# Packed attention with a gated convolution on one core: the same instructions in another written order

## The chip, the cores and the metric

The kernel runs on one core of a Trainium2 chip. The metric is the time of one execution in microseconds (us) as the device measures it. Three runs of the kernel before took 318.8, 318.99 and 320.42 us; the median is 318.99 us. A further execution was profiled; its span from the first to the last instruction is 317.6 us.

The engines are named as the profile names them: PE is the matrix engine, PEld its loading of weights, DVE the vector engine, ACT the scalar engine, POOL the general engine, SP the engine that issues the DMAs.

## The reference, cut to what matters

```python
scale = 1 / sqrt(64)                  # 8 batches, 8 heads, 576 rows, 64 columns a head; p has 32 rows
def sm_attn(qq, kk, vv):
    s = scale * matmul(qq, kk.T)
    a = exp(s - max(s)); a = a / (sum(a) + 1e-9)
    return matmul(a, vv)
pp  = sm_attn(p, k, v)                # 32 rows a head
x   = heads side by side of sm_attn(q, pp, pp)          # 576 x 512 a batch
gate = sigmoid(sum over t of conv_w[t] * x shifted back by 4 - t rows)     # 5 taps
out = (gate * (x @ w_val)) @ w_out
```

The three weight arrays come in as float64 and are turned into float32 on the chip.

## The kernel before, in words

All work is on 8 batches, one after another, each in two groups of four heads (g). The work of a batch is cut into streams, Python generators that each issue one small piece of work per step. A stream has a letter, and the batch follows it:

- `K`, `V`, `Q`, `P` issue the loads of k, v, q (two DMAs a batch, one per group, 0.59 MB each; tiles `km`, `vm`, `qm`) and of p (two small DMAs). `L` loads the weights: eight DMAs for `w_val` (0.26 MB each, tile `wv_words`), one for the taps, four for `w_out` (0.52 MB each, `wo_words`).
- `W`, `C`, `O` turn the weights from double words into float32, with ACT, DVE and POOL.
- `k` and `q` turn k and q on PE (three groups of four transposes for each g, `kpt` and `qpt`), and ACT copies them out of PSUM.
- `a` is the attention of p: scores `s` from `kT` and `pT`, a maximum (`nb`), the exponential, transposes `at`, and products `pv` with v, giving `ppd`. `p` turns `ppd` (`ppTt`).
- `s`, `t` are the second attention's scores `s` (from `qT` and `ppT`) and softmax, giving `a2`; `w` is `wp`, the product of pp with `w_val`; `x` (function `mixed`) makes the attention's output in the columns of the convolution.
- `g` (function `gate`) is the convolution: for each of four blocks of columns ACT multiplies the first tap, then DVE adds four taps, each a SCALAR_TENSOR_TENSOR that reads and writes the same tile `sig`; ACT takes the tanh.
- `v` (function `value`) makes `val` on PE, DVE multiplies it by the gate, and `gvh`/`gvl` hold the high and low part of the result. `o` (function `project`) is the product with `w_out`: 12 matmuls of 512 columns a chunk of 128 rows, and the store.

The products of `s` and `wp` use the matrix engine as eight tiles of 64 rows by 32 columns, those of `x` as tiles of 32 by 64, those of `pv` as 128 by 32. All others (transposes, `val`, `o`) use the full 128 by 128 array.

Nothing is left to a scheduler. The table `ORDER` (line 46) is a list of tokens, each a stream, its batch and a number of steps (`k0.4` is four steps of turning k of batch 0), and `run` (line 602) takes them one after another. The class `InOrder` (line 82) ties each instruction behind the one issued before it on its engine. The token list is therefore the order of every engine's queue, and of the DMAs on SP. All instructions are issued in line 90 in the kernel before, and in line 86 in the changed one, whose table is four lines shorter; groups in the profile are told apart by their tiles.

Two resources tie the streams together. PSUM holds two buffers `big` (used by `s`, `wp`, `x`, `val`), three `mid` (transposes, `pv`) and one `out`; the load buffers hold one batch of k, v and q each (two tiles, one per g), so a load of the next batch waits until the tile has been read. The sign `|` in the table ends the staging of the weights.

Of the kernel before, what the change touches and what calls it, by code (L numbers as in the profile page):

```python
# [45 lines left out]
ORDER = """
x0 L0.5 P0 W0.2 K0 W0 K0 W0 Q0 W0 P1 W0.3 V0 L0 W0 V0 Q0 W0.5 C0 L0 k0 W0 k0 P2 C0 W0 C0 W0 k0 C0 W0 C0 k0.4 K1
W0 C0 L0 k0.2 W0 k0.2 C0 W0 a0 k0 C0 W0 k0 a0 k0 K1 q0 W0 a0.2 W0 k1 q0.2 a0 k1 P3 q0.2 a0.3 L0 a0.2 Q1 a0 q0
a0.3 O0 V1 a0.7 O0 a0 O0 a0 O0.2 a0 p0 V1 O0.2 p0 O0 s0 O0 q0 w0 s0 q0 O0 s0 q0 O0 w0 s0 O0 w0 s0 q0.2 Q1 O0 t0
k1 q0 s0 k1 O0 k1 t0 s0 k1.2 K2 O0 k1 a1 t0 O0.2 s0 t0 x0 a1 O0 s0 k1 t0 a1 O0 k1.2 s0 k1.2 K2 t0 x0.2 k1 k2 P4  # L50
O0 x0 a1 O0 t0 g0 a1 q1 O0 g0 x0 a1.3 k2 g0 q1.2 a1.2 t0 q1.2 a1.2 g0 Q2 t0 x0 a1 O0 a1 q1 g0 x0.2 O0 a1 V2 g0
t0 v0 x0 O0 a1 g0 O0.2 a1 g0 q1 a1.2 O0 v0 a1.2 O0 a1 q1 g0 a1 O0.3 k2 O0 a1 p1 V2 k2.2 p1 q1 k2.2 q1 s1 g0 k2
K3 k2 O0 a2 k2 s1 k2 O0 q1 k2 a2 k2 O0.2 Q2 w1 s1 K3 q1 O0 g0 q2 s1 a2 g0 w1 O0 s1.3 w1 k2 k3 P5 O0 g0 q2.2 s1
a2 q2 x1 g0 q2 s1 | v0 a2 k3 Q3 q2 k3 v0 a2 v0 k3 s1 a2 g0 k3 a2 t1 q2 k3 a2.2 q2.2 a2 g0 a2 t1 q2 k3 v0 a2.2 k3
K4 g0 v0 k3 q2 a2 V3 k3.2 t1 Q3 g0 a2.2 g0 x1 v0 t1 g0 v0 q2 x1 t1 a2 t1 k3 x1 a2 k3 g0 t1 a2.2 x1 K4 v0 a2.2 k3
g0 v0 k4 V3 a2 a3 P6 p2 t1 p2 a3 t1 s2 v0 a3 q3 g0 q3 v0 s2 g0 x1 t1 g1 x1 v0 g1 v0 a3 x1 s2 k4 x1 g1 s2 a3 q3
k4 x1 g1 a3 q3.2 Q4 a3 w2 g1 s2 q3 v0 o0 g1 t2 g1 w2 g1 t2 k4 w2 v1 o0 g1 o0 t2 o0 g1 t2 v1 g1 v1 t2 s2 g1 x2.2
v1 g1 o0 g1 q3 a3 k4 x2 o0 s2 o0 a3 q3 g1 k4 s2 g1 s2 v1 g1 o0.2 s2 o0 v1 g1.2 t2 v1 g1 t2 a3 v1 o0 v1 a3 o0 x2
g1 a3 k4 t2 a3.2 k4 K5 v1 x2 q3 g1 a3 k4 V4 v1 a3.3 g1 k4 q3 v1.2 x2 g1 a3 q3 g2 v1 k4 a3 Q4 x2 q3 g2 v1 a3 g2
a3.2 x2 v1 x2 k4 V4 a3 g2 k4 t2 o1 K5 k4 t2 x2 g2.3 v2 o1 g2 o1 g2 a4 v2 p3 o1 p3 a4 v2 g2 a4 v2 g2 s3 o1 x3 w3  # L60
g2 o1 s3 g2 q4 s3 v2 w3 g2 s3 q4 w3 q4 o1 q4 v2 s3 g2 v2 t3 s3 o1 g2 t3 a4 o1 s3 q4 k5 o1 a4 q4 Q5 k5 g2 P7 a4.2
g2 s3 g2 t3 s3 a4 o1 k5 g2 x3 a4 o1 s3 a4 o1 t3 v2 a4 g2 x3 k5 t3 g2 v2 t3 o1.2 g2 t3 x3 v2 g2 a4 k5 a4.2 v2 t3
k5.2 v2 a4 v2 V5 k5 K6 a4 t3 x3.2 t3 a4 k5 g3 v2 x3 a4 k5 g3 k5 v2 a4 q4 g3 a4 q4 v2 o2 k5 x3 g3.2 a4 g3 x3 a4
g3 a4 x3 g3 q4 v3 V5 a4 q4 g3 o2 g3 o2.2 v3 g3 v3.2 g3 x4 g3 p4 q4 o2 g3 k5 p4 Q5 a5 k5 g3 o2 s4 q4 K6 o2 a5 s4
a5 g3 s4 g3 s4 a5 o2 w4 g3 o2 a5 g3 q5 a5.3 g3 o2 a5 g3 s4 w4 g3 q5 t4 a5 o2 s4 w4 a5 t4 k6 o2 a5 q5 k6 a5 s4 a5
q5 t4 v3 a5 V6 s4 t4 g3 s4 x4 v3 g3 q5 t4 k6 v3 Q6 s4 v3.2 q5 k6 t4 k6 x4 q5 k6.2 v3 q5 x4 t4 K7 k6 a5 v3 a5 q5
k6 t4 x4.2 q5 v3.2 t4 g4 t4 x4 a5 g4 k6 a5 k6 a5 v3 a5 x4 q5 g4 a5 x4 Q6 q5 v3 g4 k6 v3 o3 x4 g4.3 a5 o3 g4 k6
a5 a6 V6 k6 g4 o3 k7 p5 g4 o3 p5 K7 a6 g4 a6 g4 x5 a6 g4 s5 o3 g4 k7.2 o3 a6 q6 k7.2 g4 q6 o3 a6.2 s5 k7 g4 s5
v4 o3 g4 s5 o3 g4 q6 g4 v4 a6 w5 s5 g4 q6 a6 s5 t5 v4 a6 q6 w5 o3 g4 t5 Q7 q6 s5 a6 g4 q6 s5 o3 a6 k7 q6 g4 s5
o3.2 a6 k7 t5 g4 w5 t5 s5 t5 x5 o3 v4 k7 o3 t5 v4 x5 k7 t5 k7 v4 x5 k7 t5 v4 a6 x5.2 v4 x5 a6 V7 a6 g5 a6 v4 a6  # L70
g5 t5 x5 g5 a6 q6 v4 a6.2 x5 q6 g5 a6 v4 a6 t5 x5 q6 g5 a6 a7 V7 q6 Q7 v4 p6 g5 v4 a7 g5 p6 g5 a7 k7 v4 s6 k7 g5
v4 a7 q7 s6 q7.2 g5 w6 q7 v4 o4 g5 w6 a7 x6 g5 s6 a7.2 s6 w6 g5 v5 o4 g5 s6 o4 g5 s6 q7 v5 a7 o4 q7 g5 a7 v5 s6
v5 s6 v5 t6 o4 s6 o4 g5 q7 a7 o4 t6 q7 a7 s6 v5 g5 v5 t6 g5 v5.2 t6 g5 o4 t6 o4 x6 t6 a7 q7 a7 o4 x6 g5 t6 q7 v5
g5 v5 x6 o4 t6 q7 o4 v5.2 t6 g5 x6 q7 t6 x6 g5 x6 g6 v5 a7 x6 g6 x6 v5 g6 a7 x6 a7.2 v5 o5 a7 g6.2 v6 o5 g6 o5
g6 a7 o5 v6 a7 g6 v6 g6 v6.2 g6 o5.2 g6 a7 o5 g6 x7 g6 v6 a7 g6 v6 g6 a7 o5 v6 o5 g6 v6 a7 g6 p7 g6 o5 g6 v6 p7
g6 v6 g6 s7 v6 o5 v6 g6 o5 s7 g6 o5 s7 g6 s7 v6.2 w7 s7 v6 o5 t7 s7 o5 o6 w7 s7 t7 w7 t7 s7 o6 x7 t7 o6 s7 o6 t7
x7 s7 t7 x7 o6 t7 o6.2 x7.2 t7 g7 t7 g7 t7 v7 o6 g7 o6 g7 x7 g7 o6 g7.2 v7 x7 g7 v7 x7 g7 o6 v7.2 o6 x7 g7.2 o7
g7.2 v7 g7 v7 g7 v7.2 o7 g7.4 v7 g7 v7.3 o7 g7.3 o7 g7 v7.3 o7.15
"""


# [564 lines left out]
```

## Time and profile before

| | |
|---|---|
| time, median of 3 runs | 318.99 us (318.8 to 320.42) |
| span of the profiled execution | 317.6 us |
| PE busy | 284.6 us, 90% of the span, 2996 matmuls |
| DVE busy | 255.0 us, 80% |
| ACT busy | 212.7 us, 67% |
| POOL busy | 67.8 us, 21% |
| HBM read, written | 33.57 MB, 9.44 MB |

The time of the runs holds about 1.4 us more than the span of the profiled execution (318.99 less 317.6). PE's matmuls overlap, so a matmul's own duration is longer than the distance between two starts; for PE the distances between starts are read. Rows called waits give the engine and tile that stood idle, what released it, and then the sum in us, the number of waits and the longest.

### The profile page before, as it was taken

What the parts mean: (1) busy time and instruction counts of PE and PEld (TensorE: products, weight loads), DVE (VectorE), ACT (ScalarE), POOL (GpSimd) and SP (SyncE); (2) the same over time, 40 slices, a digit from 0 to 9 for tenths busy, and PEclk for the clock granted to TensorE, in tenths of its full rate; (3) what the DMA queues carried; (4) which work ended last, traced back from release to release, by engine and by line L of the source; (5) the groups of instructions that cost most, each with busy time, mean ns of one, the idle gap of its engine ahead of it and who ended that gap; (6) DMA issues with size and microseconds to landing.
All of it is one profiled execution on the core that took longest, in us unless ns stands there. A gap on an engine that the chain in (4) does not pass through costs nothing.

```text
span 317.6 us, 7342 instructions
## 1 busy us (share of the span) xinstructions
PE 284.6 (90%) x2996; PEld 209.2 (66%) x2996; DVE 255.0 (80%) x396; ACT 212.7 (67%) x432; POOL 67.8 (21%) x71
## 2 busy tenths in 40 slices
PE   0088786879989999999999999999999999999993
...
DVE  0983388679999997999789986897998977878771
...
DMA  7999999999973239533657558243702011111005
GB/s 165 216 219 254 262 240 223 217 229 188 233 150 107 68 102 238 138 95 97 151 128 196 166 135 199 85 116 103 152 33 66 35 42 60 54 70 45 33 0 166
DMA packets 42475, 43.48 MB, mean 137 GB/s; under 512 B 6085, under 2 KB 36805, under 8 KB 42442
## 3 DMA queue, kind: packets, MB, share of 16 engines
...
HBM read 33.57 MB, written 9.44 MB: 135 GB/s over the span
## 4 chain that ended last, share of the span: by engine, by line
PE 81%; ACT 8%; DMA 5%; DVE 3%; SPq 1%; issue 1%; ACTq 0%; DVEq 0%
PE o L90 32%; PE val L90 16%; PE x L90 6%; PE s L90 6%; PE kpt L90 5%; PE qpt L90 5%; PE pv L90 3%; DMA km<-in_k_dram 3%; PE at L90 3%; PE wp L90 3%; DMA wv_words<-in_moe_w_val_dram 2%; DVE sig L90 1%; ACT a1t L90 1%; ACT a L90 1%; ACT wo_top L90 1%; SPq L90 1%
## 5 line engine op out<-in xcount | busy, mean ns | idle before, releaser
L90 DVE SCALAR_TENSOR_TENSOR sig<-xp,cw,sig 128x576 f32<-128x576 f32 x128 | 106.4, 832 | 10.8 <-ACT sig L90 9.4
L90 PE MATMUL o<-woh,gvh 128*128 128x512 f32 x144 | 59.1, 411 | 0.1
L90 PE MATMUL o<-woh,gvl 128*128 128x512 f32 x144 | 56.5, 393 | 0.0
L90 PE MATMUL o<-wol,gvh 128*128 128x512 f32 x144 | 56.4, 392 | 0.0
L90 PE MATMUL val<-a2h,wph 128*128 128x288 f32 x128 | 39.4, 308 | 0.1
L90 ACT COPY osb<-o 128x512 f32<-128x512 f32 x34 | 19.8, 584 | 27.2 <-PE o L90 18.0
L90 PE MATMUL val<-a2h,wpl 128*128 128x288 f32 x128 | 37.9, 296 | 0.0
L90 PE MATMUL val<-a2l,wph 128*128 128x288 f32 x128 | 37.7, 295 | 0.0
L90 ACT ACTIVATE sig<-sig 128x576 f32<-128x576 f32 x32 | 22.0, 688 | 18.1 <-DVE sig L90 18.0
L90 POOL TENSOR_TENSOR t<-t,mx 128x576 f32<-128x576 f32 x16 | 23.1, 1442 | 47.8 <-DVE mx L90 46.6
L90 PEld LDWEIGHTS o<-woh,gvh 128*128 128x128 f32 x144 | 27.1, 188 | 9.4 <-issue 3.0
L90 POOL TENSOR_TENSOR t<-t,rs 128x576 f32<-128x576 f32 x16 | 22.0, 1372 | 50.1 <-DVE rs L90 44.6
L90 DVE SCALAR_TENSOR_TENSOR sig<-sig,val 128x576 f32<-128x576 f32 x32 | 23.9, 748 | 10.7 <-ACT sig L90 5.4
L90 PEld LDWEIGHTS o<-woh,gvl 128*128 128x128 f32 x144 | 27.1, 188 | 6.5 <-DVE gvl L90 0.4
L90 PEld LDWEIGHTS o<-wol,gvh 128*128 128x128 f32 x144 | 27.2, 189 | 4.6
L90 ACT COPY kT<-kpt 128x384 f32<-128x384 f32 x48 | 23.3, 485 | 10.2 <-PE kpt L90 10.0
L90 PE MATMUL kpt<-ident,km 96*128 96x96 f32 x192 | 26.8, 275 | 2.5 <-DMA km<-in_k_dram 2.4
L90 PE MATMUL qpt<-ident,qm 96*128 96x96 f32 x192 | 25.7, 262 | 3.2 <-ACT pT L90 1.9
L90 PEld LDWEIGHTS qpt<-ident,qm 96*128 96x128 f32 x192 | 19.6, 147 | 13.2 <-issue 7.5
L90 ACT COPY qT<-qpt 128x384 f32<-128x384 f32 x48 | 22.9, 485 | 6.9 <-PE qpt L90 6.9
L90 DVE TENSOR_TENSOR gvl<-sig,gvh 128x576 fp32r<-128x576 f32 x32 | 25.2, 788 | 2.6 <-ACT gvh L90 2.4
L90 PEld LDWEIGHTS kpt<-ident,km 96*128 96x128 f32 x192 | 21.0, 157 | 9.2 <-issue 4.9
...
## 6 DMA issues: line engine op xcount, KB each, us to landing
...
```

The source lines that it names most:

```text
L90: made = getattr(self.engine, op)(*args, **kw)
```

## The change

Only the table `ORDER` is another. The streams, the tiles, the buffers and the number of matmuls, copies and DMAs are the same. The diff is the whole table; its first lines read:

```diff
 ORDER = """
-x0 L0.5 P0 W0.2 K0 W0 K0 W0 Q0 W0 P1 W0.3 V0 L0 W0 V0 Q0 W0.5 C0 L0 k0 W0 k0 P2 C0 W0 C0 W0 k0 C0 W0 C0 k0.4 K1
+L0 K0 P0 k0.2 K0 L0 W0 k0.6 a0.2 k0.4 L0 k0 V0 k0 a0 x0 W0.9 a0.4 W0.3 a0.8 L0.2 W0.2 L0 Q0 W0.2 a0.5 W0.2 V0 q0
...
-g7.2 v7 g7 v7 g7 v7.2 o7 g7.4 v7 g7 v7.3 o7 g7.3 o7 g7 v7.3 o7.15
+v7.2 g7 o6 v7 g7 o6 g7.2 v7 g7 v7 g7.4 v7.2 g7 o6 v7.3 o7.19 o6.3
 """
```

In the lists below a row is one or more instructions that follow each other on the engine; `x8` is their number.

**SP, the start of the program.** Before:

```order
L90 DMA wv_words<-in_moe_w_val_dram 64x1024 x8
L90 DMA cw_words<-in_moe_conv_w_dram 5x1024
L90 DMA p_94<-in_p_dram 128x2x64 x2
L90 DMA km_0_100<-in_k_dram 96x4x384
L90 DMA km_1_103<-in_k_dram 96x4x384
L90 DMA qm_0_106<-in_q_dram 96x12x128
L90 DMA p_109<-in_p_dram 128x2x64 x2
L90 DMA vm_0_116<-in_v_dram 96x4x384
L90 DMA wo_words<-in_moe_w_out_dram 128x1024
L90 DMA vm_1_121<-in_v_dram 96x4x384
L90 DMA qm_1_123<-in_q_dram 96x12x128
```

Now:

```order
L86 DMA wv_words<-in_moe_w_val_dram 64x1024 x2
L86 DMA km_0_81<-in_k_dram 96x4x384
L86 DMA p_83<-in_p_dram 128x2x64 x2
L86 DMA km_1_91<-in_k_dram 96x4x384
L86 DMA wv_words<-in_moe_w_val_dram 64x1024 x4
L86 DMA vm_0_149<-in_v_dram 96x4x384
L86 DMA wv_words<-in_moe_w_val_dram 64x1024 x2
L86 DMA cw_words<-in_moe_conv_w_dram 5x1024
L86 DMA wo_words<-in_moe_w_out_dram 128x1024
L86 DMA qm_0_236<-in_q_dram 96x12x128
L86 DMA vm_1_254<-in_v_dram 96x4x384
L86 DMA wo_words<-in_moe_w_out_dram 128x1024
```

Six of the eight loads of `w_val` now stand behind the first loads of k and p, and the last two behind the first v. The last two loads of `w_out`, which stood 15th and 18th among these rows, now stand 20th and 25th.

**PE, where batch 3's `x` products stand** (`x_1_0` and `x_1_1` are the two halves of rows of group 1). Before, the two halves stand 17 rows apart, the first of them among the transposes:

```order
L90 MATMUL val_3_1966<-a2l_1277,wph_1283 128x288
L90 MATMUL at_1_0_1992<-ident,a_4_1_1837 96x128 x2
L90 MATMUL kpt_1_0_1996<-ident,km_1_1628 128x96 x4
L90 MATMUL x_1_0_2004<-a_3_1774,ppd_1243 64x288 x4
L90 MATMUL kpt_1_1_2012<-ident,km_1_1628 128x96 x4
L90 MATMUL at_1_1_2018<-ident,a_4_1_1837 96x128 x2
```

Now:

```order
L86 MATMUL at_0_2_2139<-ident,a_5_0_1863 96x128 x2
L86 MATMUL x_1_0_2148<-a_3_1778,ppd_1066 64x288 x4
L86 MATMUL x_1_1_2154<-a_3_1778,ppd_1066 64x288 x4
L86 MATMUL pv_0_2160<-vm_0_2082,a1t_0_2121 32x64 x24
L86 MATMUL s_4_1_2185<-qT_1_1981,ppT_1977 32x288 x8
L86 MATMUL qpt_0_0_2195<-ident,qm_0_2101 128x96 x4
```

The two halves stand next to each other, and `pv` and `s` follow them. Counted over PE's whole list, the array's shape changes 147 times before and 102 times now; in all 14 pairs of `x` stand directly together, where none did, and three pairs of `s` products from the same source are among the new neighbours.

**DVE, the first taps of the convolution** (`sig_1` is the second block of columns). Before:

```order
L90 RECIPROCAL sm_1_1_560<-sm_1_1_560 128x1
L90 SCALAR_TENSOR_TENSOR sig_1_660<-xp_0_78,cw,sig_1_660 128x576
L90 SCALAR_TENSOR_TENSOR sig_0_545<-sig_0_545,val_0_643 128x576
L90 SCALAR_TENSOR_TENSOR sig_1_660<-xp_0_78,cw,sig_1_660 128x576
L90 TENSOR_SCALAR wo_words<-wo_words 128x512
```

Now:

```order
L86 STREAM_TRANSPOSE a_0_399<-t_0_334 128x576
L86 SCALAR_TENSOR_TENSOR wo_top<-wo_top,wo_words 128x512
L86 TENSOR_SCALAR wo_words<-wo_top 128x512
L86 SCALAR_TENSOR_TENSOR sig_1_661<-xp_0_155,cw,sig_1_661 128x576 x4
L86 STREAM_TRANSPOSE t_1_706<-s_1_0_708 128x576
```

The four taps of a block, which had other work between them, follow each other directly. Over the whole list a tap directly follows a tap of the same block 30 times before and 55 times now.

At the end of the list, the last chunk of batch 6 (`o_3`, 12 matmuls, its copy and its store) now stands behind all of batch 7. On PE 72 matmuls of `o` follow the last `val`, where 36 did.

More of the change, by code (lines that the diff above doesn't have):

```diff
@@ L46 @@
 ORDER = """
-x0 L0.5 P0 W0.2 K0 W0 K0 W0 Q0 W0 P1 W0.3 V0 L0 W0 V0 Q0 W0.5 C0 L0 k0 W0 k0 P2 C0 W0 C0 W0 k0 C0 W0 C0 k0.4 K1
[L48 to L76, printed above, removed]
@@ L77 @@
-x7 s7 t7 x7 o6 t7 o6.2 x7.2 t7 g7 t7 g7 t7 v7 o6 g7 o6 g7 x7 g7 o6 g7.2 v7 x7 g7 v7 x7 g7 o6 v7.2 o6 x7 g7.2 o7
-g7.2 v7 g7 v7 g7 v7.2 o7 g7.4 v7 g7 v7.3 o7 g7.3 o7 g7 v7.3 o7.15
+L0 K0 P0 k0.2 K0 L0 W0 k0.6 a0.2 k0.4 L0 k0 V0 k0 a0 x0 W0.9 a0.4 W0.3 a0.8 L0.2 W0.2 L0 Q0 W0.2 a0.5 W0.2 V0 q0
+O0.8 L0 q0 Q0 W0.4 a0 q0 W0 a0 q0.2 O0.2 a0 C0 a0 C0 p0 C0 q0 p0 s0 q0 C0 s0 K1 P1 K1 Q1 O0.2 q0.3 s0 q0.2 O0 s0.2
+w0.2 O0.2 C0 t0 O0 s0 t0 O0 k1.2 O0 k1.3 w0 V1 t0 P2 k1.3 t0 k1 L0 V1 O0 k1 s0.2 C0 x0.2 k1.4 x0 t0 s0 C0 x0 C0 a1
@@ new lines @@
+s0 g0 a1.6 K2 g0 K2 a1 t0 a1.2 q1 g0 a1 g0 O0 q1.2 g0 x0 a1 q1 Q1 k2 a1 O0.2 k2 a1.2 q1.2 t0 a1 O0 a1 t0 a1.2 O0.2
+L0 a1.3 g0 a1 g0 t0 x0.2 a1 x0 p1 k2 x0 g0 p1 k2.4 g0 O0.3 k2 s1 w1.2 k2.3 g0.2 s1 K3 s1 k2 g0 P3 k2.2 a2 t0 w1 s1.2
+a2 O0 K3 q1 V2 O0 q1 a2 O0 t1 q1.4 a2 x1 a2 O0.4 v0 k3 a2 k3.4 P4 Q2 a2 t1 g0 v0 k3.2 a2 O0 t1 O0 s1 x1 k3 a2 x1
+a2.2 V2 g0 a2 s1 a2 K4 s1 O0 s1 O0.2 | g0 k3 a3.2 k3 Q2 k3.3 a3 k3 g0.2 x1 v0 a2.2 K4 v0 a2.2 v0 x1 a2 g0 a2 g0 v0
+g0 a2.2 a3 k4 g0 g1 q2 a3 v0.2 q2 a2 k4 a3.2 v0 g0 t1.2 a3.2 q2 V3 q2 a2 q2 v0 a2 s1 a3 t1 p2.2 q2 g0 a3 v0.3 k4.2
@@ new lines @@
+t1 k4 t1 k4.2 s2 g0 k4 v0 a3 K5 s2 q2 g1 a3 g1 q2.3 x1 q2.2 x1 g1.2 x1 t1.2 x1 k4 x1 k4.4 v0.2 a4 w2 a3 s2 V3 w2 K5
+a4 w2 g1.3 a4 o0 g1 o0 s2 g1 v1 o0 s2 v1 g1 Q3 v1 k4 g1 v1.2 g1 a3.2 g1 o0 v1 g1 v1 g1 P5 g1 a3 V4 a3 t2 s2 a4 o0 s2
+x2 a4 a3 P7 v1 a3.2 g1 s2 g1.2 q3 Q3 a3 o0.2 t2 v1 k5 o0.2 q3.2 a4 k5 q3 v1.2 q3.2 k5 s2 t2 k5 g1.2 a3 g1 t2 x2 a3
+x2.2 k5 x2 g1 k5 v1 k5 g2 p3 v1 P6 s2 t2 v1 k5 o0 t2 v1 k5 g2 K6 a4 q3 p3 a4 k5 V4 g2.3 a4 s3 x2 w3 o0 Q4 q3 s3.2 g2
+t2.2 g2 k5 q3 s3 q3 v1 t2 q3 t2 o1 s3 o1.2 v2 g2 k5 g2 o1 g2 v2 q3 w3.2 a4.4 g2 t3 x2.4 g2 a4 a5 o0 o1.2 s3 a4 t3 k5
@@ new lines @@
+q4 t3 q4 a5 s3 v2 a5 k5 o1 g2 x3 t3 a4.3 g2 a4.2 s3 a4.2 g2 x3.3 a4 x3 a4 q4.3 t3 q4 Q4 p4 v2.2 s3 K6 s3 p4 g2 v2
+q4.3 g3 s4 a5 t3 k6 q4.2 o1 s4 o1 k6 a5 k6 g2 k6 g2 g3 g2 t3.2 k6 g2 v2 a5 s4 o1.2 k6 v2 s4 a5 V5 g2 v2.2 g2.2 Q5 g3
+o1 v2 q4 o1 s4 a5.2 v2 a5.2 t4 a5 t3 t4 g3 x3 a5 x3.3 g3 a5 s4 q5 s4 x3 t3 g3 a5 g2 v2 v3 v2 a5 g3 k6 o1 v2 g3 q5 k6
+v3 v2 a5 k6 a5 o1 k6 g3.3 V5 w4.2 g3.2 w4 a5.3 q5 a5 q5 Q5 o2 t4 v3 x4 s4 k6.2 q5.2 k6 g3 v3 x4 o2 x4.3 g3 k6 a5 g4
+a5 a6.3 s4 Q6 g3 a6 p5.2 a6 g3 q5 t4 o2 g3 g4 k7 g4 g3.2 q5 o2 a6 o2 g3 o2 k7 g3 v3.3 g3 v3.3 g3 o2 V6 v3 o2 v3.2 t4
```

9 lines of the change are left out of this document (added).

## The prediction

> **What bounds the kernel now.** I read the page's slices first, then the busy time by stages.
>
> ```profile
> span 317.6 us, 7342 instructions
> PE 284.6 (90%) x2996; PEld 209.2 (66%) x2996; DVE 255.0 (80%) x396; ACT 212.7 (67%) x432; POOL 67.8 (21%) x71
> PE   0088786879989999999999999999999999999993
> DVE  0983388679999997999789986897998977878771
> DMA  7999999999973239533657558243702011111005
> ...
> 0.00:72.00 72.00, 46.11 (x579) 27.73 (x580) 45.77 (x76) 45.81 (x99) 28.18 (x31) 0.91 1.09 225
> 72.00:96.00 24.00, 22.22 (x322) 15.07 (x321) 23.18 (x41) 20.79 (x49) 6.48 (x6) 1.00 0.94 188
> 96.00:304.00 208.00, 207.93 (x2065) 160.16 (x2065) 181.19 (x276) 142.94 (x281) 33.17 (x35) 1.00 0.39 103
> 304.00:318.00 14.00, 8.37 (x36) 6.24 (x34) 4.87 (x7) 3.12 (x5) 0.00 (x0) 0.95 0.30 94
> ```
>
> The last four rows are windows: length, then busy us of PE, PEld, DVE, ACT and POOL, the granted clock, the DMA share and GB/s. There are three stages. Up to 72 us nobody is full but the DMA engines (share 1.09, 225 GB/s): the loads arrive one behind another and the first batches' chains are short of partners. From 72 to 96 DVE is the fullest, 23.18 of 24 us. From 96 to 304 PE works 207.93 of 208 us, so the end is set there by PE's list and by what one entry of it costs; DVE idles 26.8 us (208 less 181.19). The waits agree: what PE lost by name is at the start.
>
> ```profile
> PE pTt L90 <- DMA p<-in_p_dram: 14.1, 1, 14.1
> ACT sig L90 <- DVE sig L90: 18.0, 12, 3.3
> DVE sig L90 <- ACT sig L90: 14.7, 16, 2.0
> DVE sig L90 <- PE val L90: 5.2, 6, 2.0
> ```
>
> **Part 1: fewer changes of shape on PE.** The distance between starts tells what a change costs (timeline of PE: start, duration, count).
>
> ```profile
> 102.24 0.39 PE L90 MATMUL o<-wol,gvh 128*128 128x512 f32 x1
> 102.47 0.39 PE L90 MATMUL o<-woh,gvl 128*128 128x512 f32 x1
> 102.79 0.72 PE L90 MATMUL s<-qT,ppT 64*32 64x288 f32 x16
> 103.44 0.72 PE L90 MATMUL x<-a,ppd 32*64 32x288 f32 x8
> 104.08 0.55 PE L90 MATMUL qpt<-ident,qm 96*128 96x96 f32 x4
> ...
> 113.94 0.30 PE L90 MATMUL val<-a2h,wpl 128*128 128x288 f32 x1
> 114.08 0.29 PE L90 MATMUL val<-a2l,wph 128*128 128x288 f32 x1
> 114.30 0.71 PE L90 MATMUL x<-a,ppd 32*64 32x288 f32 x8
> ...
> 137.83 0.72 PE L90 MATMUL s<-qT,ppT 64*32 64x288 f32 x16
> 138.34 0.69 PE L90 MATMUL s<-kT,pT 64*32 64x288 f32 x16
> 138.96 0.55 PE L90 MATMUL qpt<-ident,qm 96*128 96x96 f32 x4
> ...
> L90 PE MATMUL x<-a,ppd 32*64 32x288 f32 x256 | 24.1, 447 | 0.5 <-ACT xp L90 0.5
> ```
>
> Going in: an `o` starts 0.23 after the one before it, but the `s` starts 0.32 after the last `o`; a `val` 0.14 after a `val`, but the `x` 0.22 after it. So 0.09 us. Going out: the `s` at 102.79 holds PE for 0.65 us, but the `s` at 137.83, with another `s` behind it, only 0.51. So 0.14 us. Two products put together save one way in and one way out, 0.23 us. The lists count 147 changes before and 102 now: 45 fewer, 22.5 such pairs, **5.2 us** of PE time, nearly all in the stage that PE fills. For `x` the trace has no two in a row. It runs alone in 0.64 us; one of its matmuls takes 0.447, so going out is worth between 0 and 0.19. The bounds for all: 22.5 x 0.09 = 2.0 us, and 22.5 x (0.09 + 0.19) = 6.3 us. I take what `s` shows, since `x` streams as many columns.
>
> The Trainium skill ("TensorE: Matmul & The Clock Gate", Part 3, "The mechanism") says that a weight load overlaps matmuls in flight only where the row group differs. The two `x` of a pair use the same rows, so by it a pair would save only the way in; with 14 pairs of `x` the sum would shrink by 14 x 0.14 = 2.0 us. The two `s` above also use the same rows and do save 0.14 us, so here the trace speaks against applying it to this case.
>
> **Part 2: the loads' order.** The chain of waits has two loads from issue to landing; the timeline shows who used them.
>
> ```profile
> 3.26 6.08 DMA wv_words<-in_moe_w_val_dram
> 9.35 9.81 DMA km<-in_k_dram
> ...
> 20.00:26.00 6.00, 6.00 (x56) 3.70 (x55) 3.84 (x9) 2.74 (x7) 1.29 (x1) 1.00 1.13 258
> 26.00:32.00 6.00, 4.89 (x116) 3.37 (x114) 2.04 (x7) 5.25 (x16) 0.80 (x1) 1.00 1.15 234
> ...
> 16.69 2.18 PE L90 MATMUL kpt<-ident,km 96*128 96x96 f32 x12 [1.98 <-DMA km<-in_k_dram]
> 31.17 0.43 PE L90 MATMUL pv<-vm,a1t 96*32 96x64 f32 x16 [0.41 <-ACT a1t L90]
> 32.89 0.89 PE L90 MATMUL s<-qT,ppT 64*32 64x288 f32 x16 [0.47 <-ACT ppT L90]
> 34.54 2.85 PE L90 MATMUL wp<-wv,ppT 64*32 64x512 f32 x16
> 40.37 1.21 PE L90 MATMUL s<-qT,ppT 64*32 64x288 f32 x16 [1.83 <-ACT qT L90]
> ```
>
> The fifth `wv_words` lands at 9.34, the second `km` at 19.16. Between them come three `wv_words`, the taps, p and both `km`, 2.12 MB: 216 GB/s, later about 240. With these rates the new queue lands, as an estimate: two `wv_words` at 5.7, `km_0` at 8.4, p 9.0, `km_1` 11.8, `vm_0` 19.3, `qm_0` 26.2, `vm_1` 28.7, `qm_1` 33.3. So PE starts turning k some 7 us earlier than 16.69. That gain does not last. PE's list needs `qm_0` before the last `pv`, which also needs `vm_1` at 28.7. With 1.2 us for it and the 1.7 us from 31.17 to 32.89, the first `s` of the second attention comes at about 31.5 instead of 32.89, and the second, behind `qm_1`, three transposes (2.4) and `wp` (2.8), at 38.5 instead of 40.37. What is late next is `qm_1`. I take **2.0 us**. Upper bound: the second batch's first q stands behind 8.7 MB instead of 10.0, as `w_out`'s last loads moved back: 1.3 MB at 240 GB/s, 5.5 us. Lower bound: minus 1, if the blocked transpose of q holds up what stands behind it. DVE also starts later, behind the first `s` (about 13 us), and has the conversions of `w_val` still to do. These are hidden where it idles, 2.04 busy of 6 us in the row 26 to 32; without that cover they would cost up to 5 us of DVE's time.
>
> **Part 3: DVE.** A tap directly behind a tap of the same block costs more than one with other work between.
>
> ```profile
> 72.61 0.80 DVE L90 SCALAR_TENSOR_TENSOR sig<-xp,cw,sig 128x576 f32<-128x576 f32 x1
> 73.33 0.75 DVE L90 TENSOR_REDUCE nb<-s 128x1 f32<-128x576 f32 x1
> ...
> 303.53 2.52 DVE L90 SCALAR_TENSOR_TENSOR sig<-xp,cw,sig 128x576 f32<-128x576 f32 x3
> ```
>
> After a lone tap the next instruction starts 0.72 us on; three in a row take 2.52, 0.84 each. There are 25 more such neighbours: 25 x 0.12 = 3.0 us more DVE time. Also 36 more `o` now follow the last `val`, 8.4 us at the 2.78 us per 12 that this trace gives below. PE therefore reaches the last `val` 5.2 + 8.4 us sooner, for 3.0 us more DVE work: DVE's idle time from 96 us on falls from 26.8 to 10.2 us. At its fullest, 72 to 96, it idled 0.82 of 24 us, 3.4%, which is 6.6 us over that stretch. So PE still sets the end, but narrowly, with waits between ACT, DVE and PE of the size shown in the second fence. I charge **1.5 us**; bounds 0 and 5, half of the 10.2.
>
> **Part 4: the end.**
>
> ```profile
> 154.84 2.78 PE o L90 x12
> ...
> 310.25 3.94 SPq L90 DMA_DIRECT2D out_dram<-osb  x7
> 312.40 0.58 ACT L90 COPY osb<-o 128x512 f32<-128x512 f32 x1 [0.78 <-PE o L90]
> ```
>
> SP's seven last issues end at 314.19, 1.2 us after the last copy. With 12 matmuls of the moved chunk between, only one issue is left after the last copy: **0.6 us** less, bounds 0 and 0.8.
>
> **Sum:** 317.6 - 5.2 - 2.0 + 1.5 - 0.6 = 311.3 us of span. The runs' median is 1.4 us above the profiled span, so **312.7 us**. ACT (67%) and POOL have room, and no operation is added.
>
> **Rivals.**
> - *A, the start carries over.* The loads of batch 1 and 2 pull everything forward by the full 5.5 us, `x` saves its most, DVE costs nothing: 317.6 - 6.3 - 5.5 - 0.6 + 1.4 = 306.6. For it: the DMA share of 1.09 up to 72 us. Against it: from 72 to 96 DVE was the fullest, and it has no less to do.
> - *B, the change does not do what it says.* Pairs save only the way in, the start gives nothing: 317.6 - 2.0 + 1.5 + 1.4 = 318.5. For it: no pair of `x` in this trace. Against: the pair of `s`.
> - *C, DVE becomes the bound.* DVE's list up to the last `val` is 3.0 us longer and 8.4 us of PE work stand behind it. Were DVE to keep all its 26.8 us of idle time, the span would be 317.6 + 3.0 + 8.4 - 2.0 = 327.0; each us less of idle takes one off. The forecast needs it under 12; from 17.4 on (327.0 - 9.4) the kernel is not faster. If it keeps 21.8, the span is 322.0, timed 323.4. For it: 18.0 and 14.7 us of waits between ACT and DVE at `sig`, in order on both, which taps in a row do nothing to fill. Against: these waits lie where PE, not DVE, was the bound.
>
> **How the numbers follow.** Forecast 0.57, its own range 308.5 to 317.5 (the sum with 6.3 and 3.5 us in parts 1 and 2, and with 2.0 in part 1 and 3 in part 3). A 0.17, B 0.14, C 0.12. The range 305 to 319.5 holds the forecast, A and most of B, and leaves out C and a tail. About 0.5% (1.6 us) is what a measurement of this kernel can tell from no change: faster is below 317.4, slower above 320.6. Faster: 0.55 + 0.17 + 0.04 of B = 0.76. Same: 0.02 + 0.10 + 0.01 = 0.13. Slower 0.11.
>
> **What the profile of the changed kernel would show.** Part 1: two `x` as one piece of 16 with the second start 0.45 to 0.55 us after the first; near 0.64 means B. Part 2: `kpt` starting near 10 us, but the `s` from `qT` not before 31. Part 3: DVE over 90% from 96 us to the last `val`, with no row of waits of PE on DVE above some 3 us; PE slices below 9 tenths there, with `sig` as releaser, would be C. Part 4: one store issued after the last copy. The prediction is wrong if PE's idle time moves into the middle, or if the second stage, 72 to 96 us, gets longer.

## The result, and the profile after

The changed kernel takes **322.04 us** (median of 20 runs, 320.25 to 323.71), the kernel before 320.1 us beside it (20 runs). The ratio is **1.0081**, 95% interval 1.0055 to 1.0108: slower by 0.8%, where 312.7 us, a faster kernel, was forecast. The profiled execution has a span of 321.2 us, 3.6 more than before; it is one of the longer of the 20 runs (323.39 us), so the two profiles lie further apart than the two medians, 1.9 us. The page, and the busy time in the four windows (length, then busy us of PE, PEld, DVE, ACT, POOL, the granted clock, DMA share, GB/s):

```profile
span 321.2 us, 7322 instructions
PE 286.3 (89%) x2996; PEld 216.3 (67%) x2996; DVE 263.8 (82%) x396; ACT 212.5 (66%) x432; POOL 67.0 (21%) x71
PE   0765888988699999999999999999998999999995
DVE  0375878899789899969999989898799998987840
DMA  7999999199926969334808369135104302110105
...
DVE 39%; PE 36%; ACT 14%; issue 5%; POOL 3%; DMA 2%; SPq 1%; POOLq 0%; DVEq 0%; ACTq 0%
...
0.00:72.00 72.00, 50.16 (x594) 33.37 (x602) 47.95 (x78) 47.30 (x102) 25.95 (x29) 0.91 0.96 208
72.00:96.00 24.00, 20.09 (x288) 15.12 (x275) 20.12 (x33) 18.69 (x45) 7.70 (x6) 0.93 0.83 171
96.00:304.00 208.00, 203.36 (x2074) 158.36 (x2071) 190.58 (x282) 142.82 (x281) 33.35 (x36) 1.00 0.43 110
304.00:322.00 18.00, 12.66 (x54) 9.49 (x52) 5.13 (x7) 3.71 (x6) 0.00 (x0) 0.95 0.26 87
```

Two things are to be seen. The same 396 DVE instructions are busy 263.8 us, 8.8 more than before (255.0), and the chain that ends last is now DVE's to 39%, where it was PE's to 81%. And in the long middle stage PE is no longer full: 203.36 of 208 us, where it had 207.93, while DVE's busy time rose from 181.19 to 190.58.

The balance of DVE from 96 us to the end of its last `gvl` (starts and ends of its rows in the timeline; the last one is shown) says how much of it is work and how much idle: before 184.7 us of work and 28.4 idle, after 194.3 and 18.3. The idle time did shrink, by 10.1 us. The work left at 96 us grew by 9.6, and so the last `gvl` came only 0.4 us sooner.

```profile
308.29 0.76 DVE L90 TENSOR_TENSOR gvl<-sig,gvh 128x576 fp32r<-128x576 f32 x1 [0.74 <-ACT gvh L90]
```
```profile
307.85 0.76 DVE L86 TENSOR_TENSOR gvl<-sig,gvh 128x576 fp32r<-128x576 f32 x1 [0.74 <-ACT gvh L86]
...
317.53 0.59 ACT L86 COPY osb<-o 128x512 f32<-128x512 f32 x1 [2.58 <-PE o L86]
```

Behind it stand the `o` that were moved to the end: 8.5 us from the last `gvl` to the end before (309.05 to 317.57), 12.6 after (308.61 to 321.23). That is the loss between the two profiles: -0.4 and +4.1.

Where the 8.8 us of DVE time come from is seen beside POOL. DVE and POOL, timeline rows of the changed kernel:

```profile
77.08 2.81 DVE L86 SCALAR_TENSOR_TENSOR sig<-xp,cw,sig 128x576 f32<-128x576 f32 x2
92.28 1.71 DVE L86 TENSOR_TENSOR gvl<-sig,gvh 128x576 fp32r<-128x576 f32 x1
...
75.84 1.66 POOL L86 TENSOR_TENSOR t<-t,mx 128x576 f32<-128x576 f32 x1 [2.67 <-DVE mx L86]
77.47 1.79 POOL L86 TENSOR_TENSOR wo_top<-wo_top,woh 128x512 f32<-128x512 f32 x1
79.34 1.68 POOL L86 TENSOR_TENSOR wol<-wo_top,wo_words 128x512 fp32r<-128x512 f32 x1
...
91.87 1.51 POOL L86 TENSOR_TENSOR t<-t,rs 128x576 f32<-128x576 f32 x1 [10.85 <-DVE rs L86]
```

Two taps take 2.81 us beside POOL's operations, where a pair alone takes some 1.7; a `gvl` takes 1.71 instead of 0.76. It starts 0.41 us after POOL's operation and ends 0.61 after that one's end. Over all rows I summed, for each DVE operation that overlaps a POOL TENSOR_TENSOR, what it takes above the lower quartile of its own group (its excess): 8.4 us before, 14.8 after, at nearly the same overlap (52.9 and 54.5 us). With another baseline each sum moves by about 1 us. After the change 11.7 us of it are on operations with two inputs in SBUF (taps 6.9, `gvl` 3.0, `a2l` 1.0, the addition of `eps` 0.9), and 3.2 on the conversion of the weights, 1.7 of these on TENSOR_SCALAR with one input. Operations that read `s`, `val` or `wp` from PSUM, and the reductions and transposes with one input, show none.

Which of the two starts first decides. Of the taps, `gvl` and `a2l`, 13 before and 20 after start while a POOL operation runs; they take 1.28 and 1.36 us in the mean, and end 0.62 us after POOL's operation (the median in both). Those on which POOL's operation starts later, 19 and 16, keep their length (0.77 and 0.76 us). So the order decides which DVE operations pay. The other part is a tap directly behind a tap of its block: in rows that POOL doesn't touch it is 0.84 us from start to start, against 0.73 with another operation behind it. That is near the 0.12 of the prediction; of it 0.035 us is a gap between the two that does not count as busy.

The Trainium skill ("SBUF — State Buffer", "Who interferes with whom") says that a DVE instruction with two SBUF inputs contends with a GpSimd instruction that reads SBUF, and that the order of issue decides which one blocks. The trace agrees: the 20 that start behind POOL are the ones that take 1.36 us. The TENSOR_SCALAR rows of the weights are a case that the two inputs do not explain.

### The profile page after: what moved, and what is told of

It is laid out like the page before. It is cut to its first block, busy times and chain, and to the rows that moved or that the text cites. A ratio compares the mean times of both kernels' runs of the same rounds, so it can differ in the third digit from the quotient of the medians.

```text
span 321.2 us, 7322 instructions
## 1 busy us (share of the span) xinstructions
PE 286.3 (89%) x2996; PEld 216.3 (67%) x2996; DVE 263.8 (82%) x396; ACT 212.5 (66%) x432; POOL 67.0 (21%) x71
## 4 chain that ended last, share of the span: by engine, by line
DVE 39%; PE 36%; ACT 14%; issue 5%; POOL 3%; DMA 2%; SPq 1%; POOLq 0%; DVEq 0%; ACTq 0%
DVE sig L86 21%; PE o L86 14%; PE val L86 7%; DVE gvl L86 4%; ACT sig L86 4%; PE x L86 3%; PE kpt L86 3%; PE s L86 3%; DVE sm L86 2%; PE qpt L86 2%; ACT gvh L86 2%; PE pv L86 2%; DMA p<-in_p_dram 2%; PE at L86 2%; DVE a L86 2%
## 5 line engine op out<-in xcount | busy, mean ns | idle before, releaser
L86 DVE SCALAR_TENSOR_TENSOR sig<-xp,cw,sig 128x576 f32<-128x576 f32 x128 | 110.0, 863 | 6.9 <-ACT sig L86 4.9
L86 PE MATMUL o<-woh,gvh 128*128 128x512 f32 x144 | 58.3, 405 | 0.7 <-ACT osb L86 0.6
L86 POOL TENSOR_TENSOR t<-t,rs 128x576 f32<-128x576 f32 x16 | 20.6, 1288 | 91.0 <-DVE rs L86 62.8
L86 ACT CAST gvh<-sig 128x576 fp32r<-128x576 f32 x32 | 21.7, 677 | 26.5 <-DVE sig L86 23.8
L86 POOL TENSOR_TENSOR t<-t,mx 128x576 f32<-128x576 f32 x16 | 24.0, 1499 | 69.5 <-DVE mx L86 69.5
L86 PE MATMUL val<-a2l,wph 128*128 128x288 f32 x128 | 38.5, 301 | 0.0
L86 PE MATMUL val<-a2h,wpl 128*128 128x288 f32 x128 | 38.5, 300 | 0.0
L86 DVE TENSOR_TENSOR gvl<-sig,gvh 128x576 fp32r<-128x576 f32 x32 | 27.1, 846 | 6.1 <-ACT gvh L86 5.7
L86 PEld LDWEIGHTS qpt<-ident,qm 96*128 96x128 f32 x192 | 20.8, 157 | 10.2 <-ACT qT L86 2.7
L86 PEld LDWEIGHTS val<-a2h,wph 128*128 128x128 f32 x128 | 24.7, 193 | 4.1 <-ACT a L86 1.0
L86 PEld LDWEIGHTS kpt<-ident,km 96*128 96x128 f32 x192 | 19.9, 155 | 7.8 <-ACT kT L86 1.8
```

Of the source, the lines that this page charges most:

```text
L86: made = getattr(self.engine, op)(*args, **kw)
```

## The experiments

Theories: **D**, DVE became the bound of the changed kernel, as in rival C. **L**, the new order of the loads starves the stretch from 50 to 96 us. **P**, joined `x` hold both `big` buffers. Later **C2**, POOL lengthens DVE's operations, and **S**, both orders react alike to DVE's load.

### Taps spread out

The changed kernel with steps of DVE moved between the taps; PE's list is the same.

```diff
-... k2.3 g0.2 s1 K3 s1 k2 g0 ...
+... k2.3 s1 g0 s1 g0 K3 k2 g0 ...
 (and so on through the table)
```

> The changed kernel with only the DVE list mended: steps next to a row of taps are moved between them, so that a tap directly follows a tap of the same block 31 times (changed kernel 55, before 30). PE's list is word for word that of the changed kernel. Theory D (DVE became the bound in the middle, and taps in a row made its work longer): DVE's busy time falls from 263.8 by 3 us or more, and the time falls by 2.5 to 5 us against the changed kernel, to 0.992 to 1.000 of before. Rival L (the new order of the loads starves the stretch from 50 to 96 us) and rival P (pairs of x hold both big PSUM buffers and make PE wait): within 1 us of the changed kernel, 1.005 to 1.011 of before.

Measured: 332.38 us, ratio 1.0401 (1.0349 to 1.0453), far outside every forecast. DVE's work from 96 us to its last `gvl` fell by 2.6 us (194.3 to 191.7), about what 24 neighbours fewer are worth. But DVE's gaps from 96 us to the end, summed over the timeline, are now 32.0 us instead of 19.6 (28.0 in the kernel before), 11.2 of them at `sig` behind ACT. Steps that were pulled ahead in DVE's list made it wait for inputs that weren't there yet. So the run neither confirms nor refutes that neighbours cost time; it shows that moving them costs more.

### One tap fewer, in both orders

```diff
             for kk in range(1, NT):
-                dve.scalar_tensor_tensor(acc2, shifted(x, NT - 1 - kk), ...)
+                if kk != 2:
+                    dve.scalar_tensor_tensor(acc2, shifted(x, NT - 1 - kk), ...)
```

> The kernel before with the third tap of the convolution left out in every block, 32 of DVE's 128 taps, some 25 us of DVE work; nothing else is changed. All theories: PE fills the stretch from 96 us on, so the time falls by little, 2 to 8 us, to 0.975 to 0.994 of before.

> The changed kernel with the same tap left out. Theory D: with 25 us less on DVE its list no longer sets the pace, PE's shorter list does; the time falls by 11 to 18 us to 0.95 to 0.975 of before, and this kernel is 5 us or more faster than the kernel before without that tap. Rivals L and P: what holds it is not DVE's work, so it falls by no more than the kernel before without that tap and stays at least 1 us above that one.

Measured: before 319.27 us, 0.9964 (0.9921 to 1.0008); changed 311.72 us, 0.9743 (0.9679 to 0.9807). Every theory had expected at least 0.6% in the order of before. The same 32 taps are worth nothing in the one order and 10.3 us in the other. That settles D against any cause on PE or in the loads. In the changed kernel without them the middle stage is PE's again:

```profile
96.00:304.00 208.00, 207.86 (x2084) 164.92 (x2068) 172.06 (x256) 144.12 (x282) 32.76 (x36) 1.00 0.44 109
```

With DVE relieved in both, the changed order is 7.5 us faster (319.27 less 311.72). Parts 1, 2 and 4 of the prediction were 5.2 + 2.0 + 0.6 = 7.8. A part of the 7.5 goes with the granted clock, 0.992 to 0.995 in the four runs of the changed order against 0.956 to 0.994 in the ten others: by the slopes of the last section 5 to 6 us are left at an equal clock, an estimate.

### Only the start, and only the rest

First the changed order up to the first two `x` products and then the order of before; then the reverse. The tables are cut there and the steps that remain follow in the other's order.

```diff
-x0 L0.5 P0 W0.2 K0 W0 K0 W0 Q0 W0 P1 ...        (to the second x0 product, then the rest as before)
+L0 K0 P0 k0.2 K0 L0 W0 k0.6 a0.2 k0.4 L0 ...
```

> The changed order up to the end of the first batch's first two x products (all engines, loads included), then every step that is left in the order of the kernel before; 146 changes of shape on PE, taps in a row 30 times. Theory D: 0.993 to 1.003 of before, since DVE's list from there on is the old one. Rival L: the start is what costs, 1.005 to 1.012. Rival P: 0.995 to 1.003.

> The start of the kernel before, with its order of loads, through the first two x products, and from there the changed order for all steps that remain (105 changes of shape, 56 taps directly behind a tap). Theory D: the loads are not what costs, DVE's list in the middle is; about as slow as the changed kernel, ratio to the kernel before 1.000 to 1.012. Theory L (the new order of the loads starves 50 to 96 us, and the rest is a gain): ratio 0.990 or less.

Measured: the new start 321.35 us, 1.0029 (0.9995 to 1.0063); the old start with the new rest 322.07 us, 1.0088 (1.0047 to 1.0129). The middle stage of the first, then of the second:

```profile
96.00:304.00 208.00, 207.92 (x2084) 159.11 (x2077) 181.64 (x277) 143.83 (x284) 34.73 (x36) 1.00 0.39 104
```
```profile
96.00:304.00 208.00, 203.42 (x2067) 158.83 (x2066) 190.82 (x281) 142.08 (x280) 33.72 (x36) 1.00 0.45 109
```

With the old rest, PE is full and DVE has 181.6 us; with the new rest PE has 203.4 and DVE 190.8. The loss belongs to the rest. The loads are worth nothing either way, and L falls.

### Only the pairs of x

The order of before with its 16 pairs of `x` joined, at the second's place and then at the first's; and the changed order with ten pairs taken apart.

```diff
 before, batch 3, group 1
-... k5 g3 v2 x3 a4 k5 g3 k5 v2 a4 q4 g3 a4 q4 v2 o2 k5 x3 g3.2 a4 g3 x3 a4 g3 a4 x3 g3 ...
+late:  ... g3.2 a4 g3 x3.3 a4 g3 a4 x3 g3 ...
+early: ... k5 g3 v2 x3.4 a4 k5 g3 ...
 changed
-g3 x3 a5 x3.3 g3 a5 s4 q5 s4 x3
+g3 x3 a5 x3.2 g3 a5 s4 q5 x3 s4 x3
```

> The kernel before with one thing of the change alone: in all eight batches the two x products of a group stand next to each other on PE (121 changes of array shape instead of 147, 26 fewer), DVE's list untouched. Theory D (PE's shorter list is real, and it was DVE that ate it): in the kernel before PE is the bound from 96 us on (207.93 of 208 us) and DVE idles 28 us there, so 26 x 0.115 = 3.0 us come out: 2 to 4 us faster, ratio 0.987 to 0.994, DVE's idle time from 96 on falls to 24 to 27. Theory P (joined x hold both big buffers, and that costs the val and s products behind them): no faster, ratio 1.000 or more, with more waits of PE on ACT xp.

> The kernel before with the same 16 pairs of x joined, but at the place of the first of the two: the second half is moved ahead, with its copy, where the run with the late joins moved the first half back. 26 changes of shape fewer, DVE's list untouched. Theory W (the late joins lost because the first half's xp came later, and with it the first product of the gate on ACT and the taps on DVE, which are in order): without that delay PE's saving is left, 1 to 3 us faster, ratio 0.990 to 0.997, DVE's waits on ACT sig from 96 us on at or under the 12.8 us of the kernel before. Theory P (two x hold both big buffers, whichever way they are joined): ratio 1.005 or more.

> The changed kernel with ten of its fourteen pairs of x taken apart again, the second half put behind the next full-array piece of work (122 changes of shape instead of 102), DVE's list untouched. Theory D (PE's shorter list is off the path, as DVE sets the pace): no change against the changed kernel, ratio to the kernel before 1.003 to 1.013, PE's lost time smaller by what its work grows, about 2 us. Theory P (the pairs hold both big buffers, and that is the loss): ratio 1.000 or less.

Measured: late 325.76 us, 1.0193 (1.0134 to 1.0251); early 335.86 us, 1.0472 (1.0407 to 1.0537); taken apart 326.16 us, 1.0193 (1.0126 to 1.026). All three missed what D or W expected. The first two lie where P had them, the last does not, and P's sign, waits of PE on the copy of `xp`, is all but missing in the late one (0.3 us from 96 to 304 us). A pair saves PE its 0.15 to 0.23 us, and moving the product costs more elsewhere. In the late one ACT, in order, stands at the copies of `xp` until the pair is there, 11.9 us from 96 us on where the kernel before lost 1.0 in its whole span, and everything behind it shifts. The same tanh in the kernel before, and then in this one, 2.75 us later:

```profile
124.72 0.69 ACT L90 ACTIVATE sig<-sig 128x576 f32<-128x576 f32 x1 [0.63 <-DVE sig L90]
```
```profile
124.06 0.64 ACT L89 COPY xp<-x 128x576 f32<-128x576 f32 x1 [1.19 <-PE x L89]
...
127.47 0.69 ACT L89 ACTIVATE sig<-sig 128x576 f32<-128x576 f32 x1 [0.63 <-DVE sig L89]
```

DVE's gaps from 96 us on are 33.6 us there and 44.2 in the early one, against 28.0. In the early one PE also waits 3.1 us at `x` for the copy of `xp`, which is P's wait. How much of its 15 us is the buffers and how much the shifted lists stays open. In the changed kernel taken apart, DVE's gaps are 22.1 instead of 19.6 us, so its PE list isn't wholly beside the path: it seems that a product that comes later is passed on where both engines are nearly full.

### POOL's operations taken away, and doubled

POOL's subtraction of the row maximum left out in both orders; then 32 idle POOL additions put into the changed one.

```diff
-                pool.tensor_tensor(t3, t3, m3..., op=ALU.subtract)
```
```diff
             act.mul(acc2, shifted(x, NT - 1), cw[:, c, 0:1])
+            pool.tensor_tensor(spare, same, same, op=ALU.add)     # same: ident, read four times
```

> The kernel before, without POOL's 16 subtractions of the row maximum in the second softmax (t less mx; the exponential then takes the scores as they are, everything else is computed). Pair to the next. Theory C2 (POOL's tensor operations lengthen the DVE operations that read two tiles of SBUF at the same time): the taps' mean falls from 832 to about 820 ns, DVE busy by 1 to 2 us; PE is the bound, so the time falls by 0 to 2 us. Theory T (a tap is longer because a tap of the same block is directly before it, POOL has no part): taps stay at 832.

> The changed kernel without the same 16 subtractions. Theory C2: the taps' mean falls from 863 to between 815 and 840 ns, DVE busy falls by 4 to 7 us, and since DVE is the bound here the time falls by more than in the pair: 3 to 7 us below the changed kernel's 322.0, at least 2 us more than the pair gains. Theory T: taps stay at 855 or more, and both kernels gain the same within 1 us, from the shorter chain alone.

> The changed kernel with 32 more POOL operations, one beside each block of the convolution: a sum of two constant tiles into a spare tile (128 x 512), which nothing waits for. Theory C2 (POOL's operations lengthen DVE's operations that read two tiles of SBUF): about 30 us more overlap at the 0.28 us of excess per us that the changed kernel shows (15.5 of 54.5), so DVE busy 6 to 10 us longer, the taps' mean at 890 ns or more, and as DVE sets the pace the time 4 to 9 us longer: ratio to the kernel before 1.02 to 1.04. Theory T (POOL has no part in the length of DVE's operations): DVE busy within 1.5 us of 263.8, ratio 1.004 to 1.012.

Measured: before 320.47 us, 1.0030 (0.9987 to 1.0073); changed 315.71 us, 0.9888 (0.9833 to 0.9942); with 32 more 332.85 us, 1.0400 (1.0336 to 1.0464). The additions depend on nothing and nothing waits for them. They made the taps 941 ns, DVE's busy time 276.2 us, 12.4 more, and the kernel 10.8 us slower:

```profile
PE 285.8 (87%) x2996; PEld 214.6 (65%) x2996; DVE 276.2 (84%) x396; ACT 212.0 (64%) x432; POOL 109.8 (33%) x103
...
L86 DVE SCALAR_TENSOR_TENSOR sig<-xp,cw,sig 128x576 f32<-128x576 f32 x128 | 120.0, 941 | 6.1 <-ACT sig L86 3.5 <-POOL spare L86 0.7
```

In the changed kernel the same group has 863 ns:

```profile
L86 DVE SCALAR_TENSOR_TENSOR sig<-xp,cw,sig 128x576 f32<-128x576 f32 x128 | 110.0, 863 | 6.9 <-ACT sig L86 4.9
```

That is C2 by itself. POOL's other operations do stand behind the additions in its list, but DVE did not wait longer for them: its idle time from 96 us to the last `gvl` is 17.7 us (18.3 in the changed kernel), while its work there went from 194.3 to 203.9. Taking the subtractions away gave 6.3 us in the changed order and nothing in the other, as D says. In the order of before the taps fell from 832 to 813 ns, as C2 had it. In the changed one they fell only to 856, not to 840, and T's mark was 855 or more; what speaks against T is that the two orders gained unequally, and the run with the additions. DVE's busy time fell by 4.4 us there. The rest of the gain may be the shorter way from the scores to the exponential, and the clock of those four runs (0.992 to 1.000); no run parts them.

### The last chunk ahead

```diff
-v7.3 o7.19 o6.3
+v7.3 o6.3 o7.19
```

> The changed kernel with the last chunk of o of batch 6 moved from the very end to ahead of the last batch's o. Nothing else is moved. In the changed kernel PE stands waiting for gvl at 306 us and for the out buffer at 314 us, with that chunk (2.8 us) still behind; put ahead, it fills the first wait. Expected by theory D: 1 to 2.8 us less than the changed kernel, ratio to the kernel before 0.999 to 1.006. Rival: the chunk only moves the wait, since the last gvl is what PE waits for in any case and the rest behind it is what ends last: within 0.5 us of the changed kernel, ratio 1.006 to 1.010.

Measured: 328.38 us, 1.0255 (1.0190 to 1.0320): 6.3 us slower than the changed kernel, a miss of sign. The 12 matmuls of the chunk start at 297.51, but its copy stands on ACT behind the tanh and the high part of the last block. The `out` buffer stays held till then, and PE stands still for 3.88 us, with 36 matmuls behind that need nothing from the last block. ACT, then PE:

```profile
303.65 0.68 ACT L86 ACTIVATE sig<-sig 128x576 f32<-128x576 f32 x1 [2.62 <-DVE sig L86]
305.15 0.67 ACT L86 CAST gvh<-sig 128x576 fp32r<-128x576 f32 x1 [0.82 <-DVE sig L86]
305.73 0.58 ACT L86 COPY osb<-o 128x512 f32<-128x512 f32 x1
...
306.37 0.50 PE L86 MATMUL o<-woh,gvh 128*128 128x512 f32 x1 [3.88 <-ACT osb L86]
...
308.37 0.63 PE L86 MATMUL o<-woh,gvl 128*128 128x512 f32 x1
308.80 0.63 PE L86 MATMUL o<-woh,gvh 128*128 128x512 f32 x1
...
306.40:310.00 3.60, 3.60 (x9) 2.85 (x10) 0.21 (x1) 0.00 (x0) 0.00 (x0) 0.55 0.19 73
```

After the stop, the granted clock is 0.55 for 3.6 us, and an `o` comes each 0.43 us instead of 0.23: 9 x 0.2 = 1.8 us more.

### DVE relieved without changing the result

The additions of 1e-9 taken out of both softmaxes, in both orders. Then `a2l` on POOL instead of DVE: in the changed order without those additions, and in the order of before with them.

```diff
-            dve.tensor_scalar_add(rs, rs, 1e-9)
-            dve.tensor_tensor(s3, s3, eps[:, : n * NBLK], op=ALU.add)
```
```diff
-            dve.tensor_tensor(al[:, gs], a2[:, gs], ah[:, gs], op=ALU.subtract)
+            pool.tensor_tensor(al[:, gs], a2[:, gs], ah[:, gs], op=ALU.subtract)
```

> The kernel before without the 32 small DVE operations that add 1e-9 to a sum of exponentials (the largest term of each sum is exp(0) = 1, so in float32 the addition changes nothing). Pair to the next. The groups of the changed kernel's profile give 233 and 141 ns for them, 16 of each, with the step to the next instruction about 6 us of DVE time in all. Theory D (PE is the bound here): 0 to 1.5 us faster, ratio 0.995 to 1.001. Theory S: the same gain in both kernels, within 1 us.

> The changed kernel without the same 32 additions of 1e-9. Theory D (DVE sets the pace): most of the 6 us of DVE time comes out, 3 to 6 us below the changed kernel, ratio to the kernel before 0.988 to 0.999, so that this version beats both. Theory S: the gain is that of the pair within 1 us, ratio 1.003 or more.

> The changed kernel without the 32 additions of 1e-9, and with the 16 subtractions that make a2l on POOL instead of DVE. DVE loses 12.9 us (16 x 0.807); by theory C2 the 16 x 1.3 us that POOL works more give back some 5 us as longer DVE operations, so about 8 us less DVE work. Theory D: 3 to 7 us faster than without the move (318.9), ratio to the kernel before 0.977 to 0.990, faster than both kernels. Theory S, or POOL's longer turn (a2l comes some 0.6 us later for val): ratio 0.995 to 1.005.

> The kernel before with the same 16 subtractions on POOL (the additions of 1e-9 stay). Theory D: PE is the bound and DVE's time is not what is missing; 0 to 1 us of change either way, ratio 0.996 to 1.006. Theory S: it gains as much as the changed kernel does, ratio 0.990 or less.

Measured, without the additions: before 321.82 us, 1.0087 (1.0054 to 1.0120); changed 318.92 us, 0.9992 (0.9956 to 1.0027). The changed order gains 0.9%, as D had it; the other loses 0.9%, where a small gain was expected. Of the two the changed one is now the faster. In the order of before, PE's instructions come 2.2 to 2.5 us later from 77 us to the end, at a distance that doesn't move: in the middle the DVE work that went is worth nothing. The loss lies ahead of that, where the granted clock is 0.88 up to 72 us against 0.91 in the kernel before; whether that is all of it stays open.

Measured, with `a2l` on POOL: changed 323.98 us, 1.0168 (1.0106 to 1.0231); before 321.42 us, 1.0090 (1.0052 to 1.0128). Both miss D's forecast, the first in its sign. DVE lost 12.9 us of its own work in the changed order, and yet is busy longer than without the move, 261.5 us against 258.8. The taps went from 869 to 960 ns. Without the move, then with it:

```profile
PE 280.4 (89%) x2996; PEld 212.5 (67%) x2996; DVE 258.8 (82%) x364; ACT 211.5 (67%) x432; POOL 67.3 (21%) x70
...
L86 DVE SCALAR_TENSOR_TENSOR sig<-xp,cw,sig 128x576 f32<-128x576 f32 x128 | 110.7, 869 | 7.4 <-ACT sig L86 5.4
```
```profile
PE 282.3 (88%) x2996; PEld 213.7 (66%) x2996; DVE 261.5 (81%) x348; ACT 211.4 (66%) x432; POOL 92.2 (29%) x86
...
L86 DVE SCALAR_TENSOR_TENSOR sig<-xp,cw,sig 128x576 f32<-128x576 f32 x128 | 122.4, 960 | 8.3 <-ACT sig L86 6.3
L86 POOL TENSOR_TENSOR a2l<-a,a2h 128x576 fp32r<-128x576 f32 x16 | 26.1, 1628 | 43.1 <-ACT a2h L86 43.1
```

The price that was set on POOL's 16 operations, 5 us, was a third of what they cost: 12.9 + 261.5 - 258.8 = 15.6. Of the work handed to POOL, DVE got more back than it gave.

### The maximum as a bias

```diff
-                dve.tensor_reduce(m3, t3, axis=AX.X, op=ALU.max)
-                pool.tensor_tensor(t3, t3, m3..., op=ALU.subtract)
-                act.activation(t3, t3, AF.Exp, scale=scale)
+                dve.tensor_reduce(nb, t3, axis=AX.XY, op=ALU.max, negate=True)
+                act.mul(nb, nb, scale)
+                act.activation(t3, t3, AF.Exp, bias=nb, scale=scale)
```

> The changed kernel with the second softmax's maximum taken over all 18 blocks of a partition instead of each block (any shift common to a softmax row gives the same softmax), so that it is one number a partition and goes into the exponential as its bias, by way of one small multiplication on ACT: POOL's 16 subtractions are gone, nothing is left out. Theory D with C2: like the run without the subtractions, 314 to 318 us, ratio to the kernel before 0.983 to 0.994, so that it beats both. Rival: the bias and the small multiplication put ACT's turn back as much as POOL's operation did, ratio 1.000 or more.

> The kernel before with the same maximum over a partition as a bias, POOL's 16 subtractions gone. Theory D: PE sets the pace, 0 to 1 us of change, ratio 0.997 to 1.006. Rival (the shorter chain from the scores to the exponential is the gain, whatever the order): ratio 0.990 or less.

Measured: changed 317.72 us, 0.9934 (0.9904 to 0.9965); before 322.39 us, 1.0082 (1.0043 to 1.0122). The first is faster than both kernels, by 0.7% and 1.3%. The second came out worse than forecast; its first 96 us have a clock of 0.88 and 0.87 in the two early windows, against 0.91 and 1.00, and PE's instructions are 3.0 us late at 92 us, of the 4.9 at the end. What made it slower beyond the clock stays open.

## Why the prediction was wrong

**What bounds the kernel now** was read rightly: PE, in the middle. The runs on the order of before confirm it, as taking 32 taps or 16 POOL operations away is worth nothing there.

**Part 1** was right in its price. Two `x` in a row take 1.13 us to the next piece, where two alone take 2 x 0.64 = 1.28: 0.15 for the way out, which the sum had at 0.14. The second `x` starts 0.54 us after the first, where 0.64 would have meant B. Rival B's condition is out.

```profile
118.48 1.20 PE L86 MATMUL x<-a,ppd 32*64 32x288 f32 x16
119.61 0.63 PE L86 MATMUL kpt<-ident,km 96*128 96x96 f32 x5
```

Where DVE is relieved, 7.5 us stand against the 7.8 of parts 1, 2 and 4. That they agree so well is luck in part: the new start alone gained nothing (1.0029, 0.9995 to 1.0063), so the 2.0 us of part 2 are not shown, and by the estimate above some 2 us of the 7.5 go with the clock.

**Part 2**: the loads landed within 1.2 us of the estimate, and turning k started at 9.11. The first `s` of the second attention was forecast at 31.5 and comes at 34.24, later than before (32.89), the second at 39.21 (forecast 38.5). What failed here is the chain ahead of it: PE stands at the transposes of q, which its list has ahead of the last `pv`.

```profile
9.11 2.13 PE L86 MATMUL kpt<-ident,km 96*128 96x96 f32 x12
...
25.35 0.87 PE L86 MATMUL qpt<-ident,qm 96*128 96x96 f32 x4 [1.45 <-DMA qm<-in_q_dram]
29.67 0.90 PE L86 MATMUL qpt<-ident,qm 96*128 96x96 f32 x4 [2.38 <-ACT qT L86]
30.50 1.51 PE L86 MATMUL pv<-vm,a1t 96*32 96x64 f32 x48
34.24 1.22 PE L86 MATMUL s<-qT,ppT 64*32 64x288 f32 x16 [0.47 <-ACT ppT L86]
39.21 1.16 PE L86 MATMUL s<-qT,ppT 64*32 64x288 f32 x16
```

The blocked transpose was the lower bound of that part, not its value. The first product of the gate and `val` on DVE also came at 72.16 instead of 59.91 us, which the prediction saw only as conversions that would be hidden.

**Part 3** is the step that failed: the cost of DVE's list and the idle time that DVE would keep. The forecast's own term, a tap behind a tap, was about right (0.11 us each, 0.12 forecast), but it was the only one. What POOL adds to DVE's operations was put at nothing, and measured 6.4 us more excess than before. DVE's busy time grew by 8.8 us, not 3.0, and at 96 us 9.6 us more work were left. From there on, as an estimate, 4.7 us of it are POOL's excess (3.0 before, 7.7 after), some 2 the neighbours, and 3.7 five instructions that the list before had done by then. The price of POOL next to the taps stood in the trace of before as well, where two lone taps beside POOL take 1.24 and 1.02 us instead of 0.80 (below), and end 0.61 and 0.62 us after POOL's operation; I read mean durations and took DVE's work as fixed by its list. The charge of 1.5 us, with bounds 0 and 5, rested on DVE idling down to about 11.7 us; it kept 18.3 (28.4 before). The sign that the prediction had named for being wrong came: PE's idle time from 96 us to the last `val` went from 0.1 to 4.6 us.

```profile
142.32 1.24 DVE L90 SCALAR_TENSOR_TENSOR sig<-xp,cw,sig 128x576 f32<-128x576 f32 x1
207.34 1.02 DVE L90 SCALAR_TENSOR_TENSOR sig<-xp,cw,sig 128x576 f32<-128x576 f32 x1
...
141.79 1.16 POOL L90 TENSOR_TENSOR t<-t,mx 128x576 f32<-128x576 f32 x1 [2.22 <-DVE mx L90]
206.23 1.51 POOL L90 TENSOR_TENSOR t<-t,rs 128x576 f32<-128x576 f32 x1 [2.68 <-DVE rs L90]
```

**Part 4**: one copy and one store after the last `o`, as forecast. From the end of the last copy to the end of the span it is 3.1 us instead of 4.6, more than the 0.6 of the sum, but behind 12.6 us of tail instead of 8.5.

**The sum.** The lower end of the forecast's own range, 308.5, comes out of the terms named there only with part 3 at nothing (317.6 - 6.3 - 3.5 - 0.6 + 1.4 = 308.6). The 1.4 us between span and time compare two executions; in one and the same it is about 1.8 before and 2.2 in the changed kernel's profile.

**The rivals.** C happened, and its arithmetic was the useful one: 8.4 us of `o` behind the last `val` (measured from its end to the end of the span: 13.7 us before, 21.5 after, 7.8 more), against what DVE gives up in idle time. It erred low in the work and high in the idle time kept. It also named the sign to look for, PE slices below 9 tenths in the middle; they are there at only one place (8), since the waits are short and spread; the sharper sign was DVE's share from 96 us to the last `val`, 92% after 87%. A chance of 0.12 was too little for a case whose price was 0 to 10 us on an engine that was already 87% busy in that stage.
